# A fused attention and two-layer feed-forward kernel: a new order of instructions, a products layout for GpSimd, a root moved to GpSimd

## The chip, the cores and the metric

The kernel runs on one core of a Trainium2 chip. The core has a matrix engine (TensorE, PE in the profile; its weight loads are shown apart as PEld), a vector engine (VectorE, DVE), a scalar engine (ScalarE, ACT), GpSimd (POOL) and a queue that starts the transfers (SyncE, SP). Each engine works through its own list of instructions in order; semaphores make one wait for another. The metric is the device time of one execution in microseconds, the median of several.

## The reference

The program has three parts. Attention over q, k, v of 4 batches, 8 heads, 576 positions and 64 numbers a head; then a layer with a leaky unit of its own slope for each column; then a normalised gated layer.

```python
q_d, k_d, v_d = (x.reshape(B, H, S // 4, 4, D).mean(axis=3) for x in (q, k, v))
out_up = np.repeat(sm_attn(q_d, k_d, v_d), 4, axis=2)
mask = np.abs(pos[:, None] - pos[None, :]) < 4
scores = np.where(mask, scale * np.matmul(q, k.transpose(0, 1, 3, 2)), -1e9)
out_local = np.matmul(softmax(scores), v)
x = (out_up + out_local) laid out as (2304, 512)
h = x @ w_in                                    # 512 -> 2048
x = (np.maximum(h, 0) + alpha * np.minimum(h, 0)) @ w_out      # 2048 -> 512
rms = np.sqrt(np.mean(x * x, axis=-1, keepdims=True) + 1e-06)
xn = x / rms * rms_g
g = xn @ w_gate                                 # 512 -> 1536
out = (g / (1 + np.exp(-g)) * (xn @ w_val)) @ w_out2           # 1536 -> 512
```

So each position sees the seven keys at most three places away (`out_local`), and a coarse attention over means of four positions.

## The kernel before

The 2304 tokens are cut into six blocks of 384. Each of the two layers goes over them block by block: `m1` is the first layer (`h_mm` multiplies by `w_in`, `o_mm` by `w_out`), `m2` the second (`proj` and `o_part`). Every 32-bit operand is split into two 16-bit halves (`split`: ACT writes the high half, DVE the low one), and each product is made of three 16-bit matmuls. Weights come in as 32-bit words and are decoded (`Piece.decode`: ACT, then DVE) and split before their first use.

Attention has two forms. Batch 0 and the first part of batch 1 are done densely: PE multiplies windows of 96 queries by 102 keys (`Dense`, `DenseHead`). For batch 0, `Dense.load` brings in q and k, `Dense.tr` turns them with transposes, and ACT copies the result from the matrix engine's memory into the tile `T` (line 793). The rest is done by multiplying on DVE and GpSimd (`local_tasks`): 32 stretches of positions times 4 pairs of heads lie on the 128 partitions, and a round (`g` from 4 to 11) takes 6 positions in six units, which alternate between GpSimd and DVE (`mul="GVGVGV"`). A unit multiplies q by seven keys (line 478, sums on DVE in line 489), and later the seven weights by v (line 526); line 539 adds the seven products to one row in three DVE additions. Eight rounds make 24 units on each engine.

The second layer needs one over the root of the mean square of each token. `rms_tasks` squares a block, PE sums the squares (`ssps`), DVE makes the inverse root of 128x3 numbers out of small operations (lines 1322 to 1330: a first guess by integer arithmetic, then three Newton steps; the tile is `ry`), and PE spreads it (`rps`, line 1336).

What order the instructions have on each engine is not the order of the code. `issue_order` takes the finished list, gives each instruction a cost from its engine, kind and size, plays the program forwards and backwards 40 times, keeps the best play, and fixes the order that each engine had in it. It also has an idea of when PE's clock is at half speed (`WIN`, `BUSY`, `work`).

Of the kernel before, what the change touches and what calls it, by code (L numbers as in the profile page):

```python
# [18 lines left out]
def view(ap, dims, off=0, parts=None):  # L19
    p = list(ap.ap[0]) if parts is None else list(parts)  # L20
    return bass.AP(tensor=ap.tensor, offset=ap.offset + off, ap=[p] + [list(d) for d in dims])


def issue_order(tc, nc, groups, rounds=40):
# [25 lines left out]
    def psum(a):  # L50
        return "PSUM" in str(a.tensor.space)
# [34 lines left out]
    def cost(k, ins, outs):  # L86
        i, e = insts[k], eng[k]
        if not outs:
            return 60.0
        o, n = outs[0], free(outs[0])  # L90
        if e == "SP":
            return transfer(o, ins[0])[0]
        if e == "PE":
            if wide(ins[0]) == 2:
                return n / 2.4 + (2.5 if n > 128 else 50)
            return n * 2 / 2.4 + 4 if i.is_transpose else n * 4 / 2.4 + 100
        n = max([n] + [free(a) for a in ins[:1]])
        extra = len([a for a in ins[1:] if free(a) == 1 and n > 1])
        if e == "Activation":
            return (51 if psum(ins[0]) else 93) + n / 1.2 + 93 * (extra + len(outs) - 1)  # L100
        if e == "DVE":
            if i.opcode == "Reciprocal":
                return 89 + 6.25 * n
            fast = i.opcode in ("TensorScalarPtr", "TensorCopy") and not any(psum(a) for a in ins)
            fast = fast and len([a for a in ins if free(a) > 1]) < 2
            return 89 + n / (1.92 if fast else 0.96) + 60 * (extra > 0)
        if i.opcode == "TensorTensor":
            return 148 + n * (1.667 if any(list(a.ap)[-1][0] == 0 for a in ins) else 2.104)
        return 36 + 0.83 * n if i.opcode == "Memset" else 370 + 6 * n if i.opcode == "ISA" else 200 + 2.0 * n
# [87 lines left out]
    def lag(a, b):  # L197
# [3 lines left out]
    WIN, BUSY = 3413.0, 2900  # L201
    work = [0 if eng[k] != "PE" or not aps[k][1] else
            free(aps[k][1][0]) * (1 if wide(aps[k][0][0]) == 2 or insts[k].is_transpose else 2) for k in count]
# [39 lines left out]
    for _ in range(rounds):  # L243
        end = run(succs, preds, prio, False, d)[0]
        end, seq, d = run(preds, succs, [-x for x in end], True, dur)
        prio = [-x for x in end]
        if best is None or max(end) < best[0]:
            best = max(end), seq
# [7 lines left out]
def kernel(  # L256
# [24 lines left out]
    T = 6  # L281
# [39 lines left out]
    nhalf = const.tile([128, 1], F32, name="nhalf")  # L321
    maskp = const.tile([128, 2, W, ND], F32, name="maskp")
# [53 lines left out]
    def setup():  # L376
        nc.gpsimd.memset(ident, 1.0)
        nc.gpsimd.affine_select(
            out=ident, in_=ident, pattern=[[-1, 128]], compare_op=ALU.is_equal, fill=0.0, base=0, channel_multiplier=1
        )  # L380
        nc.vector.memset(ones, 1.0)
        nc.vector.memset(nhalf, -0.5 - 2.0 ** -20)
        nc.gpsimd.iota(pidx, pattern=[[0, 1]], base=0, channel_multiplier=1)
        nc.vector.tensor_scalar(out=edge[:, 0:1], in0=pidx, scalar1=HP, scalar2=NEG, op0=ALU.is_lt, op1=ALU.mult)
        nc.vector.tensor_scalar(out=edge[:, 1:2], in0=pidx, scalar1=(NC - 1) * HP, scalar2=NEG, op0=ALU.is_ge, op1=ALU.mult)
        nc.gpsimd.memset(maskp, 0.0)
        for t in range(W):
            nc.gpsimd.memset(maskp[:, 0, t, 0:W - t], 1.0)
            nc.gpsimd.memset(maskp[:, 1, t, ND - 1 - t:ND], 1.0)
        for e in range(2):  # L390
            nc.vector.tensor_scalar(
                out=maskp[:, e], in0=maskp[:, e], scalar1=edge[:, e:e + 1], scalar2=None, op0=ALU.mult
            )
# [68 lines left out]
    def local_tasks(g, engs, tags=(None, None, None), av_pool=True, o_at=None):  # L462
# [58 lines left out]

        def mul_av(i):
# [4 lines left out]
                out=pr,  # L527
# [5 lines left out]
        def red_av(i):  # L533
# [4 lines left out]
            if av_pool:  # L538
# [180 lines left out]
    class Dense:  # L719
# [16 lines left out]
        def load(self, h):  # L736
# [3 lines left out]
            for i, (nm, x) in enumerate((("q", q), ("k", k))):  # L740
                st[nm] = t[0:TP6, i * n:(i + 1) * n]
                for j in range(2):
# [3 lines left out]
                                    ap=[[R6 * D, TP6], [D, R6], [1, D]]))  # L746
# [35 lines left out]
        def tr(self, h):  # L782
            self.alloc(h)
            st = self.st[h]
            for x, nm in enumerate(("q", "k")):
                t = st.pop(nm)
                o = st["T"][:, x, W:W + S].rearrange("d (p r) -> d r p", r=R6)
# [501 lines left out]
    def rms_tasks(m):  # L1289
# [25 lines left out]
        def ssum():  # L1315
            v_ = x1_p.tile([128, 3, NT], F32, tag="ry", name="ry")
            x, y, t_ = v_[:, 0], v_[:, 1], v_[:, 2]
            p = st["ps"][:, :, 0]
            if ne > 1:
# [3 lines left out]
            nc.vector.tensor_scalar(out=y.bitcast(I32), in0=x.bitcast(I32), scalar1=1, scalar2=None,  # L1323
                                    op0=ALU.logical_shift_right)
            nc.vector.tensor_scalar(out=y.bitcast(I32), in0=y.bitcast(I32), scalar1=-1.0, scalar2=float(0x5F3759DF),
                                    op0=ALU.mult, op1=ALU.add)
            for _ in range(3):
                nc.vector.tensor_tensor(out=t_, in0=y, in1=y, op=ALU.mult)
                nc.vector.scalar_tensor_tensor(out=t_, in0=t_, scalar=-0.5, in1=x, op0=ALU.mult, op1=ALU.mult)
                nc.vector.scalar_tensor_tensor(out=y, in0=t_, scalar=1.5, in1=y, op0=ALU.add, op1=ALU.mult)  # L1330
# [415 lines left out]
```

## Time and profile before

| | before |
|---|---|
| median of 3 runs | 968.43 us (968.34 to 970.89) |
| profiled execution | 967.56 us, span of its instructions 965.8 us |
| PE busy | 929.6 us (96%) |
| PE weight loads busy | 600.2 us (62%) |
| DVE busy | 685.5 us (71%) |
| ACT busy | 481.7 us (50%) |
| POOL busy | 117.5 us (12%) |
| mean granted clock of PE | 0.991 |

The profile gives each engine's busy time, the chain of work that ended last, groups of instructions by source line, and any stretch of the span on request. A busy PE means that some matmul is in flight. Shares over the whole span hide that the first hundred microseconds are quite another stage from the rest, so the span is best read by stretches.

### The profile page before, as it was taken

How to read it: one execution, taken by the hardware profiler on the slowest of the kernel's cores; microseconds unless marked ns; L12 is line 12 of the kernel's file. 1: busy time of each engine (PE TensorE's matmuls, PEld its weight loads, DVE VectorE, ACT ScalarE, POOL GpSimd, SP SyncE). 2: the span in 40 equal slices, each digit the busy share in tenths (PEclk: the TensorE clock that was granted, in tenths of full speed). 3: DMA queues.
4: the chain of work that ended last, by engine and by line, in shares of the span. 5: the costliest groups of instructions: out<-in, count | busy, mean ns of one | idle time of the engine just before them, and what ended most of it. 6: DMA issues, size and time to landing. Idle time of an engine off the chain costs nothing.

```text
span 965.8 us, 16581 instructions
## 1 busy us (share of the span) xinstructions
PE 929.6 (96%) x6484; PEld 600.2 (62%) x6484; DVE 685.5 (71%) x1447; ACT 481.7 (50%) x1108; POOL 117.5 (12%) x96
## 2 busy tenths in 40 slices
PE   6978999999999999999999999999999999999998
PEld 4767777799655555565566655555556666555554
DVE  4789996998999978999987899963333442542333
ACT  5999889889864273233575322221322433321322
POOL 1101100201021103333102313210000000000000
PEclk9978999999999999999999999999999999999999
DMA  8886534574302142122122211000000000000000
GB/s 207 253 274 181 161 100 137 197 226 155 128 1 58 52 141 95 44 72 62 45 85 73 82 38 36 22 22 1 20 14 1 1 1 1 1 1 10 24 1 33
DMA packets 53712, 73.80 MB, mean 76 GB/s; under 512 B 22190, under 2 KB 35138, under 8 KB 53634
## 3 DMA queue, kind: packets, MB, share of 16 engines
q1 hardware_dynamic: 53634, 72.74, 24.9%
q8 instruction: 51, 0.84, 0.4%
q14 instruction: 27, 0.22, 0.1%
HBM read 68.01 MB, written 4.72 MB: 75 GB/s over the span
## 4 chain that ended last, share of the span: by engine, by line
PE 67%; DVE 13%; ACT 9%; issue 6%; DMA 5%; POOL 0%; SPq 0%; ACTq 0%; POOLq 0%
PE gps L1488 23%; PE hps L1371 12%; PE acc L1388 12%; PE oacc L1517 11%; DMA out_dram<-ob 4%; DVE prod L539 2%; DVE ls L489 1%; ACT wr L1110 1%; ACT dls L900 1%; DVE prod L526 1%; ACT wr L1113 1%; ACT wi L373 1%; DVE ghl L374 1%; DVE prod L478 1%; DVE hps L1377 1%
## 5 line engine op out<-in xcount | busy, mean ns | idle before, releaser
L1371 PE MATMUL hps<-xt,wi 128*128 128x192 f16 (+1 forms) x1536 | 357.0, 290 | 7.2 <-DVE g L374 3.8
L1488 PE MATMUL gps<-x,w 128*128 128x384 f16 x1728 | 339.0, 326 | 3.3 <-DVE th L1499 3.0
L1388 PE MATMUL acc<-ghl,wo 128*128 128x384 f16 (+1 forms) x960 | 253.8, 310 | 1.7 <-DVE ghl L374 0.6
L1488 PEld LDWEIGHTS <-w 128*128 128x128 f16 x1728 | 169.9, 99 | 118.4 <-issue 5.2
L1517 PE MATMUL oacc<-w,uhl 128*128 128x512 f16 x630 | 191.5, 379 | 2.3 <-ACT ob L1573 1.6
L1371 PEld LDWEIGHTS <-wi 128*128 128x128 f16 x1536 | 149.5, 100 | 59.4 <-issue 7.3
L1388 PEld LDWEIGHTS <-wo 128*128 128x128 f16 x1344 | 129.0, 98 | 61.7 <-issue 4.5
L1377 DVE SCALAR_TENSOR_TENSOR hps<-g,oma,hps 128x192 f32<-128x192 f32 (+1 forms) x128 | 66.0, 516 | 61.3 <-ACT g L1375 61.0
L1497 ACT ACTIVATE th<-gps,tsc 128x384 f32<-128x384 f32 x72 | 41.8, 580 | 132.3 <-PE gps L1488 131.8
L1517 PEld LDWEIGHTS <-uhl 128*128 128x128 f16 x630 | 61.6, 98 | 67.3 <-issue 2.4
L1499 DVE SCALAR_TENSOR_TENSOR th<-th,gps 128x384 f32<-128x384 f32 x72 | 39.6, 550 | 87.8 <-ACT th L1497 87.4
L1375 ACT ACTIVATE g<-hps 128x384 f32<-128x384 f32 x96 | 47.3, 493 | 84.1 <-PE hps L1371 83.5
L1508 ACT ACTIVATE uhl<-gps 128x384 f16<-128x384 f32 x72 | 41.7, 579 | 94.3 <-DVE gps L1502 85.5
L478 POOL TENSOR_TENSOR prod<-cq,ckv 128x896 f32<-128x896 f32 x24 | 54.8, 2284 | 191.6 <-DVE ls L489 50.6
L1388 PE MATMUL acc<-g,wo 128*128 128x384 f16 (+1 forms) x384 | 70.4, 286 | 0.0
L373 ACT ACTIVATE ghl<-hps,grp 128x384 f16<-128x384 f32 (+1 forms) x73 | 42.0, 576 | 51.2 <-DVE hps L1377 48.6
L1509 DVE TENSOR_TENSOR uhl<-gps,uhl 128x384 f16<-128x384 f32 x72 | 45.3, 629 | 28.1 <-ACT uhl L1508 27.8
L526 POOL TENSOR_TENSOR prod<-ls,ckv 128x896 f32<-128x896 f32 x24 | 43.6, 1816 | 163.3 <-DVE lo L539 70.6
L539 DVE TENSOR_TENSOR prod<-prod 128x384 f32<-128x384 f32 (+1 forms) x96 | 59.4, 630 | 4.3 <-POOL prod L526 4.3
L374 DVE SCALAR_TENSOR_TENSOR ghl<-hps,grp,ghl 128x384 f16<-128x384 f32 (+1 forms) x73 | 44.3, 607 | 23.9 <-ACT ghl L373 23.6
L489 DVE TENSOR_REDUCE ls<-prod 128x14 f32<-128x896 f32 x48 | 51.1, 1075 | 0.1
L1110 ACT ACTIVATE wr<-wr 128x768 f32<-128x768 f32 (+1 forms) x48 | 41.8, 877 | 6.2 <-DMA wr<-in_moe_w_out_dram 3.2
(242 smaller groups left out, 1138.9 us busy)
## 6 DMA issues: line engine op xcount, KB each, us to landing
wr<-in_moe_w_out_dram SPq DMA_DIRECT2D x18, 512.0 KB
wr<-in_moe_w_in_dram SPq DMA_DIRECT2D x10, 768.0 KB
wr<-in_moe_w_gate_dram SPq DMA_DIRECT2D x8, 768.0 KB
wr<-in_moe_w_val_dram SPq DMA_DIRECT2D x8, 768.0 KB
ckv<-in_k_dram SPq DMA_DIRECT2D x7, 768.0 KB
ckv<-in_v_dram SPq DMA_DIRECT2D x7, 768.0 KB
wr<-in_moe_w_out_dram SPq DMA_DIRECT2D x20, 256.0 KB
sd<-in_q_dram SPq DMA_DIRECT2D x24, 144.0 KB
```

The source lines that it names most:

```text
L373: nc.scalar.activation(out=hi, in_=src, func=AF.Copy, scale=s)
L374: nc.vector.scalar_tensor_tensor(out=lo, in0=src, scalar=s, in1=hi, op0=ALU.mult, op1=ALU.subtract)
L478: engs[i].tensor_tensor(out=pr, in0=view(st["q"][:, j, t:t + TP], [[D, TP], [0, ND], [1, D]]), in1=view(st["k"][:, j, t:t + TP], [[D, TP], ...
L489: nc.vector.tensor_reduce(out=st["s"][:, j, t:t + TP], in_=st.pop(("p", i)), axis=AX.X, op=ALU.add)
L526: engs[i].tensor_tensor(out=pr, in0=view(st["s"][:, j, t:t + TP], [[ND, TP], [1, ND], [0, D]]), in1=view(st["v"][:, j, t:t + TP], [[D, TP] ...
L539: add = lambda o, a, c: nc.vector.tensor_tensor(out=o, in0=a, in1=c, op=ALU.add)
L1110: nc.scalar.activation(out=hi.bitcast(F32), in_=hi.bitcast(F32), func=AF.Prelu, scale=2.0 ** -112, alpha=2.0 ** 32)
L1371: nc.tensor.matmul(ps[:, j], wi[:, f + j, a, kk * 128:(kk + 1) * 128], x[:, b_, kk, c0:c0 + n], start=(i == 0), stop=(i == 3 * KK - 1))
L1377: nc.vector.scalar_tensor_tensor(out=ps[:, j], in0=g[:, j], scalar=oma[:, f + j:f + j + 1], in1=ps[:, j], op0=ALU.mult, op1=ALU.add)
L1388: nc.tensor.matmul(acc[e], wo_f(f)[:, a, e * 128:(e + 1) * 128], hl[:, b_], start=(f == f0 and i == 0), stop=(f == f1 and i == 2))
L1488: nc.tensor.matmul(ps, w2_t[i0 + f // 3].rearrange("p a (k c) -> p a k c", k=KK)[:, a, kk, (f % 3) * 128:(f % 3 + 1) * 128], xh[:, b_, kk] ...
L1517: nc.tensor.matmul(acc[tt], t[:, a, tt * 128:(tt + 1) * 128], w[:, b_, f % 3], start=(f in first and i == 0), stop=(f in last and i == 2))
```

## The change

1. The planner's costs are altered: a 16-bit matmul costs at least 25 ns, other matmul, ACT and small GpSimd costs differ by some nanoseconds, matmuls of a joined group count 1.5 in place of 2 as work for the clock, and the limit `BUSY` is 3000.
2. After the 40 plays, the priorities of the best one are shifted by a table `LEADS` (164 ranges of instructions, each with a number of nanoseconds), and the program is played once more; that order is used.
3. GpSimd's units of p times v write their products with the seven keys innermost (a step of 7 numbers, 28 bytes, between neighbours of `d`), and DVE adds the seven in one reduction in place of three additions. DVE's own units stay as they were.
4. The inverse root is one GpSimd operation (`pow` with -0.5) in place of eleven DVE operations; lines 1320 and 1322 stay.
5. q and k of batch 0 are loaded so that partition p holds rows p, p+96, p+192 and so on, in place of six neighbouring rows, and ACT's copy after the transposes (line 793) writes neighbouring numbers, in place of every sixth one (a step of 24 bytes).

```diff
+LEADS = (
+    (6142, 6149, 8500), (4634, 4657, 4000), (1841, 1850, 500), (2437, 2444, -500), (1116, 1482, 1000), (6896, 6972, -500),
...
             if wide(ins[0]) == 2:
-                return n / 2.4 + (2.5 if n > 128 else 50)
-            return n * 2 / 2.4 + 4 if i.is_transpose else n * 4 / 2.4 + 100
+                return max(25.0, n / 2.4 + 2.5)
+            return n * 2 / 2.4 + 3 if i.is_transpose else n * 4 / 2.4 + (128 if n < 64 else 8)
...
+        if n <= 4 and ins:
+            return 1200.0
         if i.opcode == "TensorTensor":
-            return 148 + n * (1.667 if any(list(a.ap)[-1][0] == 0 for a in ins) else 2.104)
+            return 148 + 100 * (list(o.ap)[-1][0] == 7) + n * (1.667 if any(list(a.ap)[-1][0] == 0 for a in ins) else 2.104)
...
-    WIN, BUSY = 3413.0, 2900
+    WIN, BUSY = 3413.0, 3000
...
+    lead = best[2]
+    for lo, hi, by in LEADS:
+        for k in range(lo, hi):
+            lead[k] += by
+    end, seq, d = run(preds, succs, lead, True, dur)
+    best = max(end), seq, lead
...
+        def by_key(i):
+            return engs[i] is nc.gpsimd
+
+        def over(pr, i):
+            return view(pr, [[ND * D, TP], [1, ND], [ND, D]]) if by_key(i) else pr
...
-                out=pr,
+                out=over(pr, i),
...
-            if av_pool:
+            if by_key(i):
+                nc.vector.tensor_reduce(out=st["o"][:, t:t + TP, j], in_=view(pr, [[ND * D, TP], [ND, D], [1, ND]]),
+                                        axis=AX.X, op=ALU.add)
+            elif av_pool:
...
-                                    ap=[[R6 * D, TP6], [D, R6], [1, D]]))
+                                    ap=[[D, TP6], [TP6 * D, R6], [1, D]]))
...
-                o = st["T"][:, x, W:W + S].rearrange("d (p r) -> d r p", r=R6)
+                o = st["T"][:, x, W:W + S].rearrange("d (r p) -> d r p", r=R6)
...
-            nc.vector.tensor_scalar(out=y.bitcast(I32), in0=x.bitcast(I32), scalar1=1, scalar2=None,
-                                    op0=ALU.logical_shift_right)
-            nc.vector.tensor_scalar(out=y.bitcast(I32), in0=y.bitcast(I32), scalar1=-1.0, scalar2=float(0x5F3759DF),
-                                    op0=ALU.mult, op1=ALU.add)
-            for _ in range(3):
-                nc.vector.tensor_tensor(out=t_, in0=y, in1=y, op=ALU.mult)
-                nc.vector.scalar_tensor_tensor(out=t_, in0=t_, scalar=-0.5, in1=x, op0=ALU.mult, op1=ALU.mult)
-                nc.vector.scalar_tensor_tensor(out=y, in0=t_, scalar=1.5, in1=y, op0=ALU.add, op1=ALU.mult)
+            nc.gpsimd.tensor_tensor(out=y, in0=x, in1=mhalf.to_broadcast([128, NT]), op=ALU.pow)
```

Three places show the new order. The first is the start of ACT's list. `T` is the tile that line 793 (845 after) fills, one number for each pair of heads; `wr` is a weight being decoded, by lines 1110 and 1113 (1162 and 1165 after); `dd` and `dls` are the exponentials of the two attentions. Before:

```order
L793 ACTIVATE T_183<-tps 128x3x96 x4
L793 ACTIVATE T_188<-tps 128x3x96 x3
L825 ACTIVATE dd,dsum<-sps,dm 72x144 x2
L793 ACTIVATE T_188<-tps 128x3x96
L825 ACTIVATE dd,dsum<-sps,dm 72x144 x2
L1110 ACTIVATE wr<-wr 128x768
L793 ACTIVATE T_198<-tps 128x3x96
L1113 ACTIVATE wr<-wr,nhalf 128x768
```

And after the change, at the same place of ACT's list:

```order
L845 ACTIVATE T_185<-tps 128x288 x4
L1162 ACTIVATE wr<-wr 128x768
L1165 ACTIVATE wr<-wr,nhalf 128x768
L845 ACTIVATE T_190<-tps 128x288 x4
L877 ACTIVATE dd,dsum<-sps,dm 72x144 x4
L952 ACTIVATE dls,dlsum<-lsps,dlm 96x102 x8
L845 ACTIVATE T_200<-tps 128x288
```

The first half of the first weight is now decoded ahead of the second pair of heads.

The second place is the start of SP's list of transfers: `wo` is the room that q and k of batch 0 are loaded into, `wr` again a weight of `w_in`, `sdv` v for the coarse attention. Before:

```order
L743 DMA wo_107<-in_q_dram 96x6x64 x2
L743 DMA wo_107<-in_k_dram 96x6x64
L1650 DMA rows_174<-in_moe_alpha_dram 16x128
L1650 DMA rows_174<-in_moe2_rms_g_dram 4x128
L743 DMA wo_107<-in_k_dram 96x6x64
L743 DMA wo_107<-in_q_dram 96x6x64
L1091 DMA wr_661<-in_moe_w_in_dram 128x2x768
```

After, from the same transfer on (the seventh of the list):

```order
L795 DMA wo_108<-in_q_dram 96x6x64
L1143 DMA wr_663<-in_moe_w_in_dram 128x2x768
L795 DMA wo_108<-in_q_dram 96x6x64
L795 DMA wo_108<-in_k_dram 96x6x64
L803 DMA sdv_160<-in_v_dram 72x2x512
L1695 DMA rows_176<-in_moe_alpha_dram 16x128
```

The first half of a weight is the eighth transfer, where it was the thirteenth.

The third place is DVE's list around the inverse root of the second block (`ry`); `th`, `gps` and `uhl` are the gated unit of the second layer, on which PE waits. Before:

```order
L1322 TENSOR_SCALAR ry<-ssps 128x3
L1252 TENSOR_SCALAR tsc<-eb_117,rg_116 128x1
L1256 SCALAR_TENSOR_TENSOR inv_122<-eb_117 128x1
L1323 TENSOR_SCALAR ry<-ry 128x3
L1499 SCALAR_TENSOR_TENSOR th<-th,gps 128x384
L1258 TENSOR_SCALAR inv_122<-inv_122,rg_116 128x1
L1325 TENSOR_SCALAR ry<-ry 128x3
L1502 SCALAR_TENSOR_TENSOR gps<-th,gps 128x384
L1328 TENSOR_TENSOR ry<-ry 128x3
```

After:

```order
L1374 TENSOR_SCALAR ry<-ssps 128x3
L1167 SCALAR_TENSOR_TENSOR wc<-wr 128x768
L1547 SCALAR_TENSOR_TENSOR gps<-th,gps 128x384
L1310 TENSOR_SCALAR inv_123<-inv_123,rg_117 128x1
L1554 TENSOR_TENSOR uhl<-gps,uhl 128x384
L404 TENSOR_SCALAR s_115<-allps 128x1
L1544 SCALAR_TENSOR_TENSOR th<-th,gps 128x384
```

Eleven `ry` operations, which stood between the others, are gone from DVE's list.

## Rows read from the trace of the kernel before

**Rows 1.** Page, part 4: the chain that ended last, shares by engine.
```profile
PE 67%; DVE 13%; ACT 9%; issue 6%; DMA 5%; POOL 0%; SPq 0%; ACTq 0%; POOLq 0%
```

**Rows 2.** Stretches: length, busy us of PE, PEld, DVE, ACT, POOL, clock, DMA, GB/s.
```profile
0.00:60.00 60.00, 47.70 (x352) 37.67 (x352) 35.85 (x109) 45.75 (x134) 6.93 (x30) 0.94 0.83 238
60.00:110.00 50.00, 40.34 (x439) 34.63 (x440) 46.91 (x113) 47.49 (x131) 8.27 (x12) 0.90 0.63 183
110.00:260.00 150.00, 148.91 (x1515) 123.44 (x1513) 133.22 (x309) 133.78 (x284) 14.79 (x10) 1.00 0.52 163
260.00:340.00 80.00, 76.22 (x447) 43.75 (x446) 78.78 (x169) 37.57 (x69) 12.95 (x6) 1.00 0.16 48
...
420.00:480.00 60.00, 57.82 (x360) 35.19 (x359) 58.42 (x113) 22.28 (x54) 19.36 (x9) 1.00 0.13 39
...
640.00:880.00 240.00, 239.37 (x1429) 140.52 (x1428) 92.10 (x182) 70.75 (x140) 0.00 (x0) 1.00 0.02 4
880.00:965.80 85.80, 79.91 (x445) 43.20 (x443) 29.89 (x43) 23.44 (x33) 0.00 (x0) 1.00 0.06 19
```

**Rows 3.** PE's waits: line, what it waited for, us, times, longest.
```profile
PE hps L1371 <- DVE g L374: 3.8, 5, 1.6
...
PE gps L1488 <- DVE th L1499: 3.0, 4, 1.0
```

**Rows 4.** ACT groups by form: busy us, mean ns, idle before.
```profile
L793 ACT ACTIVATE T<-tps 128x288 f32<-128x288 f32 x16 | 10.4, 694 | 10.0 <-PE tps L792 10.0
L687 ACT ACTIVATE aT<-atps 72x288 f32<-72x288 f32 x24 | 9.3, 404 | 1.6 <-PE atps L685 1.2
```

**Rows 5.** ACT in order of time, first eviction and first decode.
```profile
8.20 1.18 ACT L793 ACTIVATE T<-tps 128x288 f32<-128x288 f32 x2 [6.11 <-PE tps L792]
...
17.86 0.90 ACT L1110 ACTIVATE wr<-wr 128x768 f32<-128x768 f32 x1
```

**Rows 6.** SP in order of time, seventh transfer and first weight half.
```profile
4.99 1.31 SPq L743 DMA_DIRECT2D wo<-in_q_dram  x2
...
9.38 0.63 SPq L1091 DMA_DIRECT2D wr<-in_moe_w_in_dram  x1
```

**Rows 7.** Stretch 10 to 20 us, columns as in rows 2.
```profile
10.00:20.00 10.00, 9.28 (x56) 6.36 (x54) 5.72 (x21) 6.96 (x18) 0.64 (x1) 1.00 1.00 251
```

**Rows 8.** DVE groups by form, sums of the products.
```profile
L539 DVE TENSOR_TENSOR prod<-prod 128x256 f32<-128x256 f32 x48 | 31.4, 653 | 0.0
L539 DVE TENSOR_TENSOR prod<-prod 128x384 f32<-128x384 f32 x48 | 29.1, 607 | 4.3 <-POOL prod L526 4.3
...
L539 DVE TENSOR_TENSOR lo<-prod 128x128 f32<-128x128 f32 x48 | 18.3, 381 | 0.0
```

**Rows 9.** Lines 489 and 539 alone: shortest, median, longest ns, first and last start.
```profile
L489 DVE TENSOR_REDUCE ls<-prod x48: 1066/1075/1086, 188.5 to 618.4; 128x14 f32<-128x896 f32 x48
...
L539 DVE TENSOR_TENSOR prod<-prod x96: 405/543/2166, 229.6 to 641.1; 128x384 f32<-128x384 f32 x48, 128x256 f32<-128x256 f32 x48
```

**Rows 10.** Line 539 alone by stretch: DVE busy (count), clock, DMA.
```profile
260.00:340.00 80.00, 12.75 (x24) 1.00 0.16 48
420.00:480.00 60.00, 18.82 (x36) 1.00 0.13 39
```

**Rows 11.** Tile ry alone by stretch: PE, PEld, DVE busy.
```profile
260.00:340.00 80.00, 1.15 (x6) 1.06 (x6) 3.35 (x12) 1.00 0.16 48
...
sum 965.80, PE 7.12 PEld 6.19 DVE 13.65; mean PE 0.59 PEld 0.52 DVE 1.14
```

**Rows 12.** DVE in order of time, second block's root, first and last.
```profile
269.14 0.14 DVE L1322 TENSOR_SCALAR ry<-ssps 128x3 f32<-128x3 f32 x1
...
281.57 0.15 DVE L1330 SCALAR_TENSOR_TENSOR ry<-ry 128x3 f32<-128x3 f32 x1
```

**Rows 13.** POOL groups by form.
```profile
L526 POOL TENSOR_TENSOR prod<-ls,ckv 128x896 f32<-128x896 f32 x24 | 43.6, 1816 | 163.3 <-DVE lo L539 70.6 <-issue 58.8 <-DVE ls L520 33.9
...
L833 POOL TENSOR_TENSOR dd<-dd,dsum 72x576 f32<-72x576 f32 x4 | 4.9, 1220 | 37.3 <-DVE dsum L832 20.7 <-ACT T L793 16.6
```

More of the change, by code (lines that the diff above doesn't have):

```diff
@@ L21, in view @@
     return bass.AP(tensor=ap.tensor, offset=ap.offset + off, ap=[p] + [list(d) for d in dims])
+LEADS = (
[28 rows of a table added]
+)
 def issue_order(tc, nc, groups, rounds=40):
@@ L99, in cost @@
         if e == "Activation":
-            return (51 if psum(ins[0]) else 93) + n / 1.2 + 93 * (extra + len(outs) - 1)
+            return (61 if psum(ins[0]) else 103) + n / 1.2 + 93 * (extra + len(outs) - 1)
         if e == "DVE":
@@ L200, in issue_order @@
     engines = sorted(set(eng))
-    WIN, BUSY = 3413.0, 2900
+    WIN, BUSY = 3413.0, 3000
     work = [0 if eng[k] != "PE" or not aps[k][1] else
-            free(aps[k][1][0]) * (1 if wide(aps[k][0][0]) == 2 or insts[k].is_transpose else 2) for k in count]
+            free(aps[k][1][0]) * (1 if wide(aps[k][0][0]) == 2 or insts[k].is_transpose else
+                                  1.5 if k in joined else 2) for k in count]
     def run(P, S, prio, fwd, d):
@@ L243, in issue_order @@
     for _ in range(rounds):
-        end = run(succs, preds, prio, False, d)[0]
-        end, seq, d = run(preds, succs, [-x for x in end], True, dur)
+        lead = [-x for x in run(succs, preds, prio, False, d)[0]]
+        end, seq, d = run(preds, succs, lead, True, dur)
         prio = [-x for x in end]
         if best is None or max(end) < best[0]:
-            best = max(end), seq
+            best = max(end), seq, lead
[3 more added lines that the diff above has]
+            lead[k] += by
+    end, seq, d = run(preds, succs, lead, True, dur)
+    best = max(end), seq, lead
     info = mybir.DependencyInfo(mybir.DependencyClass.NoSync, mybir.DependencyReason.DATA)
@@ L321 @@
     nhalf = const.tile([128, 1], F32, name="nhalf")
+    mhalf = const.tile([128, 1], F32, name="mhalf")
     maskp = const.tile([128, 2, W, ND], F32, name="maskp")
@@ L381, in setup @@
         nc.vector.memset(ones, 1.0)
+        nc.gpsimd.memset(mhalf, -0.5)
         nc.vector.memset(nhalf, -0.5 - 2.0 ** -20)
@@ L1315, in ssum @@
         def ssum():
-            v_ = x1_p.tile([128, 3, NT], F32, tag="ry", name="ry")
-            x, y, t_ = v_[:, 0], v_[:, 1], v_[:, 2]
+            v_ = x1_p.tile([128, 2, NT], F32, tag="ry", name="ry")
+            x, y = v_[:, 0], v_[:, 1]
             p = st["ps"][:, :, 0]
```

27 rows, old and new, of the table LEADS are left out of this document.

## Prediction

> **What bounds the kernel now.** I read the chain of waits first, for who is on the path, then busy time by stretch, then what PE waits for, then single lines. The chain is 67% PE, 13% DVE, 9% ACT [rows 1]: mostly the matrix engine, but the rest is large enough to ask where it sits. The stretches say it [rows 2]. From 640 to 880 us PE is busy for 239.37 of 240 us: nothing but less matmul work could help there, and the change takes no matmul away. From 110 to 260 us it is 148.91 of 150. The holes are elsewhere. In the first 60 us PE is idle for 12.3 us, from 60 to 110 us for 9.7; in that second stretch ACT is busy for 47.49 of 50 us and DVE for 46.91, so PE is fed by two engines that are both full, while weights are decoded and the first attention runs. From 260 to 340 us PE idles 3.78 us with DVE busy for 78.78 of 80, and from 420 to 480 us 2.18 us with DVE at 58.42 of 60: there DVE alone is the bound. In the last stretch, 5.9 us are idle, mostly around the last stores. So of the span of 965.8 us some 22 us are open at the start, 7 us in the middle (3.78, 2.18 and 1.09), and the tail is untouched. The longest waits of PE have the same face: its matmuls of the first layer wait for DVE's split `g`, 3.8 us, and those of the second for DVE's gate `th`, 3.0 us [rows 3].
>
> **Part by part.** *The product and its sum (point 3).* A GpSimd unit costs DVE three additions now, with means of 607, 653 and 381 ns [rows 8], 1.64 us. The reduction that takes their place reads 896 numbers, as line 489 does, whose 48 cases lie between 1066 and 1086 ns [rows 9]; here 7 neighbours go into each sum where there 64 do, but what is read is as much. I take 1.08. It saves 0.56 us for each of 24 units, 13.5 us. The means of line 539 hold waits: the shortest of its two-input additions is 405 ns and the longest 2166, while line 489, with one input, never leaves 1.09, and runs beside the same GpSimd products [rows 9]. So the saving is largest where DVE is fullest: from 260 to 340 us, 24 additions (8 units, half of them GpSimd's) took 12.75 us, 1.59 a unit; from 420 to 480 us 36 took 18.82, 1.57 [rows 10]. That is 4 x 0.51 = 2.0 us in the one stretch and 6 x 0.49 = 2.9 us in the other.
>
> On GpSimd the product's write gets a step of 28 bytes. Before it took 1816 ns [rows 13]. No row shows GpSimd writing with a step, so bounds: no change below, and above the ratio of ACT's copy with a step of 24 bytes to its like without one, 694 to 404 ns [rows 4], hence 3.1 us. I take 1.9: the nearest row is that of the same instruction, and its reads stay. POOL is busy for 19.36 of 60 us in its fullest stretch shown [rows 2]; 12 products there at worst add 15 us to it. What pays is only DVE waiting for a product, 4.3 us over the whole run now [rows 8].
>
> [...]
>
> *The root (point 4).* The tile `ry` has 13.65 us of DVE in all; seven operations of about 0.16 us stay, so 12.5 us go, and 3.35 - 0.15 = 3.2 us of them from 260 to 340 us [rows 11]. There the root's first and last operation are 12.4 us apart, since other work is queued between them [rows 12]. The single GpSimd operation is not in the trace. A small one has to cost at least nearly nothing, and at most what 576 numbers cost, 1220 ns [rows 13], if a power is no dearer than a long product; I take 1 us. It stands behind GpSimd's products in order, at most one of about 2 us is ahead of it, so it comes in 3 us at worst, where 12.4 us passed before. No loss.
>
> In the two holes DVE so gets 2.0 + 3.2 = 5.2 us for 3.78 us of idle PE, and 2.9 for 2.18. Part of these waits is the way from PE over ACT and DVE back, which no saving shortens, but the new order can put other matmuls there. Of 7 us open in the middle I take 5, bounds 0 and 7. The saving outside the holes (some 18 us) is worth nothing: PE is full there.
>
> *The copies of batch 0 (point 5).* 16 copies of 694 ns become like line 687, 404 ns [rows 4]: 4.6 us of ACT within the first 40 us or so. Each transfer still moves pieces of 64 numbers, so loads cost what they did. *The order (points 1 and 2)* shows at the start. ACT decodes the first weight half ahead of the second pair of heads, and the later splits of `w_in` move up too. How far can that go? ACT's first copy is at 8.20 us [rows 5], set by the load. Of its 14.25 idle us up to 60, 6.0 are behind that; it has 2.5 idle from 60 to 110. With the 4.6 us saved, 13 us is the most. From the other side, DVE has nothing less to do in the first 110 us, and is idle for only 3.1 us in the second stretch [rows 2], so it can hold PE where it was: 0. I take 5 us, the copies in full and a little for the order, as ACT is the fuller of the two. PE's granted clock is 0.94 and 0.90 in these two stretches and 1.00 in all others [rows 2], so the altered clock count can matter only there; with PE waiting for ACT and DVE in them I give it no term, and 10% of 50 us, 5 us, bounds it on both sides.
>
> Where the order is moved elsewhere PE is full, and another order changes nothing there; where PE is idle at the end nothing is moved that it waits for: 0.
>
> **Sum.** 965.8 - 5 - 5 = 955.8 us of span; the profiled execution has 1.76 us around its span, and the median is 0.87 us over it: 958.4, I say 958.5 us.
>
> **Rivals.** *The start stays.* DVE, not ACT, feeds PE from 60 to 110 us; then the decode that comes earlier only waits longer, and the middle alone counts: 968.4 - 5 = 963.4 us. For it: DVE at 46.91 of 50 and the wait on DVE's `g`. Against it: DVE's own stretch begins only when ACT has copied and decoded.
>
> *Nothing moves.* The waits of PE in the middle are latency, not lack of DVE, and the start is DVE's: 968 us. For it: 7 us of idle PE are many small holes of 1 us or so. Against it: they lie just where DVE is over 97% busy.
>
> *Slower: ACT stuck behind an early weight.* The first half of `w_in` is now the eighth transfer and stands in ACT's list ahead of the second pair's four copies. Before, it was issued at 9.38 us [rows 6] and first touched at 17.86 [rows 5]; the eighth place is issued near 5.6 us. The transfers are saturated from 10 to 20 us at 251 GB/s [rows 7], so a half of 768 KB takes 3.1 us, and the two halves moved up push the loads of q and k back by 6.3 us. ACT can do nothing else while it waits for the half. If all of this reaches the path and the middle gives 2 in place of 5: 968.4 + 6.3 - 2 = 972.7 us. It decides where the half lands after the first four copies and the loads behind it, that is from about 14 us on: from there each us moves the start by one. Against it: the total loaded before PE is full is the same, and the decode is work that must be done anyway.
>
> *That the change does not do what it says*: the table shifts numbers, and the listed order does show the moves; not a case of its own.
>
> **Chances.** Forecast 55%, its own range 952 to 962; the start stays 20%; nothing moves 13%; slower 12%. A change of 0.3% (2.9 us) is what a measurement of this kernel can tell from none, so faster means below 965.5, slower above 971.3. Forecast and most of the second case (18 of 20) are faster: 73%; the third with the rest: 15%; slower 12%. The range from 949 to 970 takes in the bounds of both terms short of their ends together and the third case, and leaves out the slower one and part of the unlikely gain.
>
> **What would show it.** Right: the copies of line 845 at about 0.4 us; PE's idle time from 0 to 110 us at 17 us or so, where it was 22; reductions of 1.08 us that do not stretch beside GpSimd; DVE's total near 660 us; PE idle for about 2 us in the middle holes. [...]

## The result and the profile after

The changed kernel takes 958.6 us (median of 4 runs, 957.6 to 959.53), the kernel before 968.39 in the same comparison: a ratio of 0.9885, 95% interval 0.9867 to 0.9903. The medians are 9.8 us apart; by the ratio, in which the experiments are compared, it is 11.1 us. Of one experiment, e5, two of six executions took 5346 and 1362 us, the profiled one among them, and are left out of its ratio. The forecast was 958.5 us. The number was met; the experiments below say that the reason behind it was mostly not.

The profiled execution took 958.69 us, with a span of 957.0 us, 8.8 us less than before. The chain that ended last (part 4 of the page of after, shares by engine) has moved from the feeding engines to PE, compared with [rows 1]:

```profile
PE 78%; ACT 4%; DMA 3%; DVE 3%; issue 1%; SPq 0%; ACTq 0%
```

Busy time by stretch of after, columns as in [rows 2]:

```profile
0.00:60.00 60.00, 50.17 (x344) 37.55 (x344) 38.20 (x107) 45.06 (x136) 7.10 (x31) 1.00 0.89 239
60.00:110.00 50.00, 41.53 (x471) 36.65 (x472) 47.59 (x128) 47.33 (x134) 5.30 (x10) 0.93 0.64 191
110.00:260.00 150.00, 147.39 (x1495) 121.67 (x1493) 133.09 (x287) 134.45 (x282) 20.41 (x14) 1.00 0.48 153
260.00:340.00 80.00, 79.50 (x484) 46.45 (x483) 77.01 (x159) 42.68 (x90) 13.63 (x7) 1.00 0.25 80
...
420.00:480.00 60.00, 59.13 (x377) 36.74 (x375) 57.27 (x103) 25.52 (x63) 15.13 (x7) 1.00 0.15 41
480.00:640.00 160.00, 159.93 (x1001) 95.00 (x999) 138.57 (x241) 62.71 (x157) 41.20 (x22) 1.00 0.19 55
640.00:880.00 240.00, 240.00 (x1430) 140.66 (x1429) 86.84 (x156) 71.22 (x140) 1.70 (x2) 1.00 0.02 4
```

PE's idle time up to 110 us is 9.83 + 8.47 = 18.3 us, where it was 22.0. The hole from 260 to 340 us has shrunk from 3.78 to 0.50, that from 420 to 480 from 2.18 to 0.87; from 110 to 260 one has grown from 1.09 to 2.61. Each of these is one execution; the table of experiments shows that the 18.3 us of the start vary by some 2.5 us between executions of one order. The granted clock of the first stretch is 1.00 (was 0.94), of the second 0.93 (was 0.90).

PE's waits on DVE have changed less than the holes (waits of after: what PE waited for, us in all, times, longest, as [rows 3]); the wait for `th` is not among them any more:

```profile
PE hps L1416 <- DVE g L416: 4.3, 4, 2.5
PE tps L844 <- DMA wo<-in_q_dram: 4.1, 2, 3.0
```

ScalarE's first copies and decodes, in order of time (start, us, engine, line; in brackets the idle time before it and what ended it), against [rows 5]; the first half of `w_in`, now the eighth transfer, was issued at 4.53 us; before it was the fourteenth, not the thirteenth, and issued at 9.38 us [rows 6]:

```profile
7.56 0.71 ACT L845 ACTIVATE T<-tps 128x288 f32<-128x288 f32 x2 [5.49 <-PE tps L844]
...
11.42 0.89 ACT L1162 ACTIVATE wr<-wr 128x768 f32<-128x768 f32 x1 [1.73 <-DMA wr<-in_moe_w_in_dram]
...
15.79 0.89 ACT L845 ACTIVATE T<-tps 128x288 f32<-128x288 f32 x2 [2.01 <-PE tps L844]
```

The instructions themselves, groups by form of after (busy us, mean ns, idle before), against [rows 4, 8, 13]:

```profile
L845 ACT ACTIVATE T<-tps 128x288 f32<-128x288 f32 x16 | 6.2, 408 | 10.0 <-PE tps L844 9.9
...
L575 POOL TENSOR_TENSOR prod<-ls,ckv 128x896 f32<-128x896 f32 x24 | 47.9, 1997 | 126.4 <-issue 54.8 <-DVE lo L588 27.0 <-DVE ls L563 26.2
L1375 POOL TENSOR_TENSOR ry<-ry,mhalf 128x3 f32<-128x3 f32 x6 | 7.0, 1170 | 242.3 <-DVE ry L1374 242.3
...
L588 DVE TENSOR_REDUCE lo<-prod 128x128 f32<-128x896 f32 x24 | 25.8, 1075 | 0.0
L591 DVE TENSOR_TENSOR prod<-prod 128x384 f32<-128x384 f32 x24 | 17.9, 747 | 0.0
L591 DVE TENSOR_TENSOR prod<-prod 128x256 f32<-128x256 f32 x24 | 14.0, 581 | 0.0
L591 DVE TENSOR_TENSOR lo<-prod 128x128 f32<-128x128 f32 x24 | 7.0, 291 | 0.0
L575 DVE TENSOR_TENSOR prod<-ls,ckv 128x896 f32<-128x896 f32 x24 | 37.6, 1565 | 0.0
L521 DVE TENSOR_TENSOR prod<-cq,ckv 128x896 f32<-128x896 f32 x24 | 31.1, 1294 | 0.0
```

Additions and reductions together are 64.7 us, where the additions alone were 78.8: 14.1 less. But DVE's own products, the last two rows, took 14.9 us less before:

```profile
L526 DVE TENSOR_TENSOR prod<-ls,ckv 128x896 f32<-128x896 f32 x24 | 25.9, 1079 | 0.0
L478 DVE TENSOR_TENSOR prod<-cq,ckv 128x896 f32<-128x896 f32 x24 | 27.9, 1162 | 0.0
```

DVE's total went from 685.5 to 676.8 us only.

### The profile page after: what moved, and what is told of

It is laid out like the page before. It is cut to its first block, busy times and chain, and to the rows that moved or that the text cites. A ratio compares the mean times of both kernels' runs of the same rounds, so it can differ in the third digit from the quotient of the medians.

```text
span 957.0 us, 16449 instructions
## 1 busy us (share of the span) xinstructions
PE 928.3 (97%) x6484; PEld 599.6 (63%) x6484; DVE 676.8 (71%) x1333; ACT 481.4 (50%) x1108; POOL 128.0 (13%) x103
## 4 chain that ended last, share of the span: by engine, by line
PE 78%; ACT 4%; DMA 3%; DVE 3%; issue 1%; SPq 0%; ACTq 0%
PE gps L1533 26%; PE acc L1433 16%; PE hps L1416 16%; PE oacc L1562 14%; DMA out_dram<-ob 3%; PE avps L749 1%; PE sps L709 1%; PE atps L737 1%; DMA wr<-in_moe_w_gate_dram 1%; ACT wr L1165 1%; ACT w L415 1%; DVE prod L575 1%; PE xps L612 1%; DVE hps L1422 1%; DVE wc L1167 0%
## 5 line engine op out<-in xcount | busy, mean ns | idle before, releaser
L1416 PE MATMUL hps<-xt,wi 128*128 128x192 f16 (+1 forms) x1536 | 345.9, 289 | 6.6 <-DVE g L416 4.3
L1533 PE MATMUL gps<-x,w 128*128 128x384 f16 x1728 | 349.5, 326 | 0.6 <-ACT x L1447 0.4
L1433 PE MATMUL acc<-ghl,wo 128*128 128x384 f16 (+1 forms) x960 | 249.4, 310 | 0.5 <-ACT ghl L415 0.4
L1562 PE MATMUL oacc<-w,uhl 128*128 128x512 f16 x630 | 200.4, 379 | 1.8 <-ACT ob L1618 1.7
L575 POOL TENSOR_TENSOR prod<-ls,ckv 128x896 f32<-128x896 f32 x24 | 47.9, 1997 | 126.4 <-issue 54.8
L1547 DVE SCALAR_TENSOR_TENSOR gps<-th,kap,gps 128x384 f32<-128x384 f32 x60 | 37.1, 618 | 9.6 <-PE gps L1533 7.0
```

The lines of the kernel that those rows point to most:

```text
L575: engs[i].tensor_tensor(out=over(pr, i), in0=view(st["s"][:, j, t:t + TP], [[ND, TP], [1, ND], [0, D]]), in1=view(st["v"][:, j, t:t + TP], ...
L1416: nc.tensor.matmul(ps[:, j], wi[:, f + j, a, kk * 128:(kk + 1) * 128], x[:, b_, kk, c0:c0 + n], start=(i == 0), stop=(i == 3 * KK - 1))
L1433: nc.tensor.matmul(acc[e], wo_f(f)[:, a, e * 128:(e + 1) * 128], hl[:, b_], start=(f == f0 and i == 0), stop=(f == f1 and i == 2))
L1533: nc.tensor.matmul(ps, w2_t[i0 + f // 3].rearrange("p a (k c) -> p a k c", k=KK)[:, a, kk, (f % 3) * 128:(f % 3 + 1) * 128], xh[:, b_, kk] ...
L1562: nc.tensor.matmul(acc[tt], t[:, a, tt * 128:(tt + 1) * 128], w[:, b_, f % 3], start=(f in first and i == 0), stop=(f in last and i == 2))
```

## The experiments

In e1 to e3, e5, e6 and e9 to e12 each engine's order is fixed: the planner's search is taken out and lists of instruction numbers are put in. Where one instruction takes the place of several, it stands where the last of them stood (GpSimd's root where its input is planned to be ready); several stand where the one stood.

```diff
-    prio, d, best = [float(-k) for k in count], dur, None
...
-    best = max(end), seq, lead
+    best = 0, {e: fixed_order(x) for e, x in ORDER.items()}
```

All ratios are to the kernel before, run on the same chip in the same comparison; one hundredth is 9.7 us. The idle times of PE are those of one profiled execution. In the first column of them after, e3, e6, e12 and e1 have the same instructions in the same order, but for the copies: their 18.3 to 20.8 us show how far executions differ, and differences of 2.5 us there say nothing. That of e2 comes from its fastest execution, 965.53 us.

| kernel | ratio, 95% interval | PE idle 0-110 | PE idle 110-640 |
|---|---|---|---|
| before | 1 | 22.0 | 7.7 |
| after | 0.9885 (0.9867 to 0.9903) | 18.3 | 4.2 |
| e1 order alone | 1.0034 (1.0019 to 1.0049) | 20.0 | 12.1 |
| e2 edits, old order | 0.9995 (0.9980 to 1.0011) | 20.3 | 8.9 |
| e3 strided copies | 0.9905 (0.9888 to 0.9923) | 19.8 | 4.3 |
| e4 no table | 1.0001 (0.9990 to 1.0013) | 20.1 | 12.5 |
| e5 product back | 0.9940 (0.9921 to 0.9958) | - | - |
| e6 root back | 0.9991 (0.9969 to 1.0013) | 20.8 | 9.7 |
| e7 early shifts | 1.0009 (0.9996 to 1.0021) | 18.6 | 10.5 |
| e8 late shifts | 1.0241 (1.0227 to 1.0255) | 16.9 | 30.5 |
| e9 before, searched | 0.9947 (0.9931 to 0.9962) | 24.9 | 6.5 |
| e10 after, searched on | 0.9945 (0.9924 to 0.9966) | 22.4 | 5.6 |
| e11 all keys innermost | 0.9952 (0.9934 to 0.9971) | 23.7 | 7.0 |
| e12 split product | 0.9896 (0.9874 to 0.9918) | 20.0 | 3.5 |

**e1, the order without the instructions.** The code of before, with ORDER from the changed kernel.

> The computation of before (strided copies, three additions per unit, the root on VectorE), with the instructions of every engine in the order of the changed kernel; where one instruction stands for several, the several stand in its place. Pieces theory (the prediction's sum): the order alone gives little at the start, since the copies still cost 4.6 us more of ScalarE, and nothing in the middle; 966 us, PE idle from 0 to 110 us at 21 us and from 110 to 640 us at 7 us. Order theory (the searched order does it, and the cheaper instructions are only fewer): 960 us or less, with PE idle from 0 to 110 us at 18 us.

972.99 us: slower than before. Both theories had it faster. The order found for the changed kernel is worse than the old order when the instructions are the old ones. The root's eleven operations stand in one block here, as in e6 below, and share in this. DVE's products take 68.9 us, as in after, though all additions of before are there:

```profile
L634 DVE TENSOR_TENSOR prod<-ls,ckv 128x896 f32<-128x896 f32 x24 | 39.7, 1656 | 0.0
L586 DVE TENSOR_TENSOR prod<-cq,ckv 128x896 f32<-128x896 f32 x24 | 29.2, 1216 | 0.0
```

**e2, the instructions without the order.** The changed code, with ORDER from the kernel before.

> The changed computation (contiguous copies, one reduction per GpSimd unit, the root on GpSimd), with every engine's instructions in the order of the kernel before. Pieces theory: 960 us; the start gives the 4.6 us of the copies and the middle 3 to 5 us. Order theory: 966 us or more, because in the old order the instruction that PE waits for comes no earlier when another one is shorter.

968.71 us, no change. The pieces theory, which is the prediction's sum, falls here: contiguous copies, cheaper sums and the short root together gain nothing while the order is the old one. The two kernels' rows, e1 and then e2, for 0 to 110 and 110 to 640 us (columns as in [rows 2]):

```profile
0.00:110.00 110.00, 89.98 (x792) 72.44 (x793) 84.49 (x226) 93.02 (x258) 11.04 (x38) 0.97 0.74 215
110.00:640.00 530.00, 517.89 (x3795) 341.34 (x3794) 476.32 (x982) 295.17 (x678) 103.56 (x57) 1.00 0.29 89
```

```profile
0.00:110.00 110.00, 89.73 (x839) 74.61 (x840) 86.41 (x235) 93.61 (x277) 15.14 (x43) 0.92 0.80 223
110.00:640.00 530.00, 521.14 (x3793) 342.44 (x3791) 477.28 (x901) 291.49 (x662) 110.37 (x58) 1.00 0.29 88
```

In e2 DVE executes 102 instructions fewer from 110 to 640 us than before (901, was 1003) and PE still idles for 8.9 us; that what PE waits for stands no earlier in the queues would explain it, but is not shown wait by wait. DVE's products take 54.5 us, as before (53.8):

```profile
L583 DVE TENSOR_TENSOR prod<-cq,ckv 128x896 f32<-128x896 f32 x24 | 27.9, 1162 | 0.0
L637 DVE TENSOR_TENSOR prod<-ls,ckv 128x896 f32<-128x896 f32 x24 | 26.6, 1106 | 0.3
```

The additions that are left, those of DVE's 24 units, took 49.4 us (21.1, 17.4 and 10.9), 2.06 a unit where the mean of before was 1.64.

**e3, the copies.** The changed kernel's order; only the copies are undone.

```diff
-                                    ap=[[D, TP6], [TP6 * D, R6], [1, D]]))
+                                    ap=[[R6 * D, TP6], [D, R6], [1, D]]))
...
-                o = st["T"][:, x, W:W + S].rearrange("d (r p) -> d r p", r=R6)
+                o = st["T"][:, x, W:W + S].rearrange("d (p r) -> d r p", r=R6)
```

> The changed kernel in its own order, with the loads and the 16 copies of batch 0 as before (ScalarE writes with a step of 24 bytes). Copies theory: the start loses what the prediction gave to the copies, 4 to 5 us, so 963 us, with PE idle from 0 to 110 us at 22 us. Order theory: ScalarE's copies wait for transfers anyway at the start, so the longer ones are hidden in part: 959 to 960 us.

960.58 us; 0.9905 against 0.9885 makes 2 us, and the intervals overlap, so it may be nothing. The copies took 705 ns again (10.2 us in all, 4.0 more), and before them ScalarE still waits 9.6 us for PE's transposes. PE's idle time to 110 us shows no price either: 19.8 us here and 20.0 in e1 with the slow copies, 20.0 in e12 and 20.8 in e6 with the fast ones, all in the same order.

**e4, no table.** `LEADS = ()`; the planner's new costs stay.

> The changed kernel with the planner's new costs and all its cheaper instructions, without the table of priority shifts. Pieces theory: within 2 us of the changed kernel, 959 to 961 us. Order theory: the shifts carry most of the gain, 964 to 968 us, with PE idle more than 20 us from 0 to 110 us.

970.05 us, as before the change. The table of shifts carries 11 us (1.0001 against 0.9885), all of the gain in this kernel. A higher clock of PE alone does not bring the gain: the mean granted clock is 0.998 here, the highest of all beside e6's, and 0.996 in after. From 110 to 640 us:

```profile
110.00:640.00 530.00, 517.47 (x3799) 340.52 (x3798) 472.94 (x896) 292.99 (x670) 111.83 (x61) 1.00 0.29 89
```

DVE's work is that of after (896 instructions, 909 there), and PE idles for 12.5 us in place of 4.2.

**e5 and e6, product and root undone in the changed kernel's order.**

```diff
-            return ... if by_key(i) else pr
+            return ... if False else pr
...
-            if by_key(i):
+            if False:
```

> The changed kernel in its own order, but for the 24 GpSimd units VectorE adds with three instructions, in the place of the one reduction, and GpSimd writes the products without a step. Pieces theory: the middle loses the product's share of 5 us, some 3 us, so 961.5 us. Fitted-order theory (the order alone was 14 us above the changed kernel and the copies account for 2 of it; an order searched for these durations is spoilt where VectorE's instructions between are longer): 12 us are left for product and root together, by VectorE's time 13.5 to 12.5, so 964 to 965 us, with PE idle some 5 us more from 110 to 640 us.

0.9940, 5.3 us over the changed kernel; the 3 us of the one theory and the 6 of the other both lie within the intervals. Where the time is lost is not shown: there is no profile of an undisturbed execution.

```diff
-            nc.gpsimd.tensor_tensor(out=y, in0=x, in1=mhalf.to_broadcast([128, NT]), op=ALU.pow)
+            ... (the 11 operations of before)
```

> The changed kernel in its own order, with the second layer's root by 11 VectorE instructions in the place where the input of GpSimd's one is made, six times. Pieces theory: the middle loses the root's share of 5 us, some 2.5 us, so 961 us. Fitted-order theory: 964 to 965 us. Since each root's 11 instructions follow one on the other on VectorE, the loss would stand where the first root is, between 200 and 300 us, and from 420 to 640 us.

968.06 us: 10 us lost, for 11.9 us of DVE (13.0 in place of 1.08 for `ry`). In this kernel the 11 stand one behind the other, where other work lay between them before, so it is the root and its place together. PE's idle time from 110 to 640 us rises from 4.2 to 9.7, 2.6 of it from 480 to 640 us, where after has almost none:

```profile
480.00:640.00 160.00, 157.31 (x993) 93.85 (x992) 141.00 (x264) 65.59 (x171) 38.14 (x20) 1.00 0.19 56
```

e6 has the matmuls of after in the same order, so their starts can be compared one by one. Just before the first root they are 1.8 us later than in after, at 640 us 8.4 us later, in steps from 200 to 225, at 271, and from 480 to 570 us: 6.6 us of this profiled execution's loss stand at the roots.

e3, e5 and e6 lose 2, 5 and 10 us, 17 in all; e1, with all three undone, 14.4.

**e7 and e8, one part of the table.**

```diff
-        for k in range(lo, hi):
+        for k in range(lo, hi) if lo < 2400 else ():      # e8: lo >= 2400
```

> The changed kernel with only those 55 of the 164 shifts that begin at an instruction number under 2400, which are planned up to about 200 us. The whole table was worth 11.5 us against none. Start theory: most of its worth is in the first 200 us, where weights are decoded, so 962 us or less. Spread theory: the holes that the table closes lie all along to 640 us, and each shift was chosen in a plan that holds the others, so the part is worth 3 to 5 us: 965 to 967 us.

> The changed kernel with only those 109 of the 164 shifts that begin at an instruction number of 2400 or more, planned from some 150 to 230 us on. Start theory: 967 us or more. Spread theory: 963 to 966 us; early and late part together then gain about the 11.5 us of the whole table. If both parts give nearly nothing, the shifts work only together.

969.87 and 991.77 us. Neither theory had a loss of 23 us; the last sentence of the second expectation comes nearest: the shifts work only together. The late part alone tears a hole, e8 from 240 to 260 us, PE busy for 3 of 20 us while it waits for ScalarE's `w` and DVE's `ghl` (columns as in [rows 2] and [rows 3]):

```profile
240.00:260.00 20.00, 3.00 (x17) 1.95 (x15) 18.60 (x35) 14.22 (x17) 2.77 (x1) 0.59 0.46 148
```

```profile
PE allps L391 <- ACT w L1176: 10.3, 2, 8.2
PE acc L1433 <- DVE ghl L416: 6.6, 1, 6.6
```

**e9, e10, e11, orders searched anew.** Ranges of instructions were shifted in priority and a shift kept if the plan ended earlier, with equal effort: e9 for the computation of before (three parts undone as in e3, e5, e6), e10 from the changed kernel's table on, e11 with

```diff
         def by_key(i):
-            return engs[i] is nc.gpsimd
+            return av_pool
```

> The computation of before (strided copies, three additions per unit, the root on VectorE) in an order that was searched for it as the changed kernel's was searched for its own: priority shifts of ranges of instructions on the changed kernel's planner costs and clock count, each kept only if the plan ends earlier. Search theory (the gain is the searched order, and the cheaper instructions are worth little in themselves): 955 to 960 us, as fast as the changed kernel. Interaction theory (the order pays only with the cheaper instructions: order alone 973 us, instructions alone 968.7): 964 us or more, since VectorE still has the 25 us more to do in the stretches where it is over 97% busy.

> The changed kernel's computation, its order searched on from the table of 164 shifts in the same way and with as much search. Search theory: 954 to 957 us, and within 3 us of the computation of before with its own searched order. Interaction theory: 954 to 957 us, and 8 us or more ahead of it. If the table had been used up: 958 to 959 us.

> As the run before, but VectorE's 24 units too have their products with keys innermost and one reduction for three additions, with an order searched for that. If VectorE's write with a step of 28 bytes costs what GpSimd's did (1.997 for 1.816 us, 10%), a product takes 1.2 us undisturbed, the reduction saves 0.54 us of 1.62 a unit, VectorE has some 10 us less in all, and the time is 951 to 956 us. If it costs what ScalarE's step of 24 bytes did (694 for 404 ns), a product takes 1.9 us, VectorE has 6 us more than now, and the time is 958 to 965 us.

963.6, 963.78 and 966.11 us. e9 is just short of the interaction theory's 964 us: the old instructions, in an order made for them, are 5 us faster than before. e10 was to be faster than after by either theory and is 5 us slower: shifts that each made the plan end earlier made the kernel end later. But with the same search the old and the new computation end alike (0.9947, 0.9945), where the interaction theory had them 8 us apart. The rows of e9, then of e10:

```profile
0.00:110.00 110.00, 85.14 (x788) 70.35 (x788) 81.43 (x223) 92.34 (x252) 12.08 (x41) 0.94 0.75 211
110.00:640.00 530.00, 523.45 (x3853) 346.51 (x3854) 471.62 (x1005) 296.42 (x687) 102.95 (x56) 1.00 0.30 91
```

```profile
0.00:110.00 110.00, 87.64 (x784) 70.12 (x784) 84.26 (x227) 89.52 (x258) 10.29 (x39) 0.97 0.77 215
110.00:640.00 530.00, 524.39 (x3856) 346.50 (x3856) 474.14 (x906) 295.89 (x682) 116.63 (x62) 1.00 0.29 90
```

In the middle e9 keeps PE as full as e10 does (6.5 and 5.6 us idle), with three additions a unit and the root on DVE; both idle more at the start than after's order does in any of its five profiles. Idle time is not all that an order changes: over the whole span e9 idles 38.2 us, before 36.2; e9 is faster since PE is busy for 923.0 us in place of 929.6, with the same number of matmuls. Why is not shown. e11's two kinds of product, GpSimd's and DVE's (shortest, median, longest ns):

```profile
L642 POOL TENSOR_TENSOR prod<-ls,ckv x24: 1813/1832/3359, 237.8 to 624.1; 128x896 f32<-128x896 f32 x24
L642 DVE TENSOR_TENSOR prod<-ls,ckv x24: 1768/1782/3003, 239.4 to 625.9; 128x896 f32<-128x896 f32 x24
```

DVE pays for the 28-byte step nearly what ScalarE did for its 24 bytes: 1.64 times (1782 for 1085 ns in after), where that was 1.7 (694 for 408). It is the second case of the expectation, and 966 us lies just past the 965 given there. But DVE did not get the 6 us more of that case: it is busy for 672.0 us, 676.8 in after, so this does not explain the time.

**e12, GpSimd's product in two halves.**

```diff
-            engs[i].tensor_tensor(
-                out=over(pr, i),
...
+            n = 1 if by_key(i) else TP
+            for u in range(0, TP, n):
+                engs[i].tensor_tensor(
+                    out=over(pr, i)[:, u:u + n],
...
```

> The changed kernel in its own order, but each of GpSimd's 24 products of probabilities and values is issued as two instructions of half the size, one after the other. Port theory (a VectorE product with two inputs waits until the GpSimd instruction that runs has ended; that is where 15 of the 25 us that VectorE was to save went): the GpSimd halves take about 1 us, VectorE's product of the same kind falls from a mean of 1565 to about 1330 ns with its longest near 2.1 us (2.78 now), and the time is 957.5 to 959.5 us. Shared-rate theory (the two engines slow each other as long as both run): the mean stays at 1.5 us or more.

959.19 us, no different from after. DVE's products and GpSimd's halves:

```profile
L647 POOL TENSOR_TENSOR prod<-ls,ckv 128x448 f32<-128x448 f32 x48 | 57.4, 1254 | 121.5 <-issue 55.3 <-DVE ls L633 26.3 <-DVE lo L660 23.7
...
L647 DVE TENSOR_TENSOR prod<-ls,ckv 128x896 f32<-128x896 f32 x24 | 33.5, 1395 | 0.0
```

The mean wait of a DVE product falls from 480 to 307 ns (1565 and 1395 less the medians, 1085 and 1088), as the first theory of the expectation has it. The longest is still 2725 ns (2781 in after), but it stands behind a product of q and k, which was not split; behind a split one no DVE product takes more than 1.83 us. The longest, and one behind the first of two halves (the row of POOL holds both):

```profile
549.38 2.07 POOL L591 TENSOR_TENSOR prod<-cq,ckv 128x896 f32<-128x896 f32 x1 [2.47 <-issue]
549.67 2.73 DVE L647 TENSOR_TENSOR prod<-ls,ckv 128x896 f32<-128x896 f32 x1
...
244.04 2.76 POOL L647 TENSOR_TENSOR prod<-ls,ckv 128x448 f32<-128x448 f32 x2 [6.60 <-PE allps L461]
244.15 1.77 DVE L647 TENSOR_TENSOR prod<-ls,ckv 128x896 f32<-128x896 f32 x1
```

The longest half of GpSimd's took 1869 ns, where the median is 1031, and this pair 2.76 us, where the pair at 303.62 us, during which DVE had no product, took 1.90: DVE gets in between the halves, and the second half waits in its turn. DVE has 8.5 us less to do (668.3 for 676.8) and the end does not move.

## Why the number was right and the reasons were not

*What bounds the kernel* was read rightly as to place: the holes at the start and in the middle closed by 3.7 us and by 3.5 (7.7 to 4.2), the full stretch stayed full, the tail stayed. Of the 3.7 some 2.5 can be chance, since the other executions of this order idle up to 20.8 us there.

*The product and its sum.* The durations held: reductions of 1.07 us that never stretch, 14.1 us of additions saved for 13.5, products of 2.0 us on GpSimd for 1.9. The 15 us that it allowed for in GpSimd's fullest stretch counted 12 products; 6 of the 12 units there are GpSimd's. The median of its product rose from 1714 to 1837 ns, 7%. The step that failed is "What pays is only DVE waiting for a product, 4.3 us": DVE pays in another way. A product of its own with two inputs that meets one on GpSimd can wait inside its own duration. In after, POOL and DVE from 310 us on:

```profile
310.19 1.82 POOL L575 TENSOR_TENSOR prod<-ls,ckv 128x896 f32<-128x896 f32 x1 [1.56 <-DVE lo L591]
```

```profile
310.49 2.34 DVE L575 TENSOR_TENSOR prod<-ls,ckv 128x896 f32<-128x896 f32 x1
```

2.34 us for 1.08: the excess of 1.26 us is near the 1.52 that GpSimd still had to go. In after 14 of DVE's 48 products wait so (1.36 to 2.96 us): each takes its own 1.08 us and, less 0.1 to 0.3, what GpSimd's product still had to go; the 24 that overlap with none take 1.09 at most. It goes the other way too: six of DVE's products took 1.08 or 1.09 us, and the GpSimd product that each of them met took 2.62 to 3.40, where the medians of its two kinds are 1.84 and 2.09. Why one waits for the other the traces do not show. Which instructions wait is set by the order: DVE's products take 53.8 and 54.5 us in the old one (before, e2), 68.7 and 68.9 in the new one (after, e1), with either instructions. In e2 the waits went to the additions that were left. So "DVE's total near 660 us" was missed by 17: here taking instructions out did not take the waits out.

*The root.* 1.17 us on GpSimd for the 1 taken, and PE never waits for `rps`. Its worth was mis-sized: "The saving outside the holes (some 18 us) is worth nothing: PE is full there". e6 shows that in the new order, with the operations in one block, much of the root's DVE time is on the path: 10 us by the ratio, 6.6 of them seen at the roots in its profile. A good part of that stands from 200 to 225 and from 480 to 570 us, in stretches that were full in the trace of before (148.91 of 150 us from 110 to 260, 159.36 of 160 from 480 to 640).

*The copies.* 408 ns for 404. Their price, 4.6 us of the start term, was at most some 2 (e3), and PE's idle time at the start shows none. That the longer copies lie in ScalarE's waits for PE is likely, but only argued.

*The order* is the term that failed outright. It was given "a little" at the start and, elsewhere, "another order changes nothing there: 0". e4 puts 11 us on the table, and e1 and e2 say how: order alone 1.0034, instructions alone 0.9995, both 0.9885. There are no two terms of 5 us to add; with this order there is one of 10 us that both have to be there for. That the sum came to the same was luck, helped by the fact that it priced the same holes. The clock was given no term, and a higher one does not bring the gain by itself: e4 and e6 have the highest mean, 0.998, and are no faster than before.

*The rivals.* ScalarE does wait for the early half, 1.73 us until 11.42; the 2.01 us before the copy at 15.79 are a wait for PE's transposes. The half landed before the 14 us from which that case decided. "The start stays" and "nothing moves" did not come. Nothing moves is, however, what the changed kernel without its table does.

*What stays open.* Whether the old instructions would reach 958.6 us too with a table as good as the change's: the search made here gave 963.6 for them and 963.8 for the new ones, so these two orders show no worth of the instructions, and the last 5 us belong to the order of the change; a better one for the old instructions was not found. One searched order of each is little to go by: e10's search, which began at the change's own table, moved the end by 5 us the wrong way. Also open is what in the 164 shifts closes the holes: halves of the table gain nothing (e7) or lose (e8), and no single shift was followed. And why e10, planned to end earlier, idles 22.4 us at the start, 1.6 more than the longest of the five executions of after's order there (18.3 to 20.8).

## What to carry to other kernels

Where an order is planned or searched for the whole program, cross the two: new instructions in the old order, old instructions in the new one. Here a saving on an engine that is full in a stretch was worth nothing in the old order (e2), and an order made for one set of durations was worse than the one it replaced for another (e1). Give both sides the same search before a saving is called worth its time: here old and new instructions then came out alike (e9, e10). And look at several executions before a difference of 2 us in the idle time of one stretch is believed. A hole in PE says where time can be won, not which part of a change will win it.

## What the hardware showed that was not expected

The same product on GpSimd in the kernel before, and in after GpSimd's, DVE's and DVE's reduction (shortest, median, longest ns, first and last start in us):

```profile
L526 POOL TENSOR_TENSOR prod<-ls,ckv x24: 1687/1714/2928, 227.9 to 634.5; 128x896 f32<-128x896 f32 x24
```

```profile
L575 POOL TENSOR_TENSOR prod<-ls,ckv x24: 1817/1837/2677, 224.6 to 629.9; 128x896 f32<-128x896 f32 x24
L575 DVE TENSOR_TENSOR prod<-ls,ckv x24: 1074/1085/2781, 228.0 to 636.8; 128x896 f32<-128x896 f32 x24
L588 DVE TENSOR_REDUCE lo<-prod x24: 1070/1074/1081, 231.4 to 633.6; 128x128 f32<-128x896 f32 x24
```

A write with a step of 28 bytes costs GpSimd 7% in the median (1714 to 1837 ns), but DVE 64% (1085 to 1782 ns, e11), much as ScalarE pays for its 24 bytes (408 to 694 ns, 70%). DVE's reductions, with one input, are untouched by GpSimd (8 of the 72 begin while one of its products or powers runs, and take 1.09 us at most), while its two-input products of p and v reach 2.8 us. And a power of 3 numbers a partition takes GpSimd 1.17 us in the mean, near the 1220 ns of its product of 576 numbers [rows 13].
